# Bulk weights on ScalarE's DMA queue in fewer pieces, x first, another planned order, in a sliding-window attention block

## The chip, the cores and the metric

The kernel runs on 1 core of a Trainium2 chip, as one launch. The metric is the device time of that launch in microseconds (us), lower is better. The kernel before was run 13 times: median 338.93 us, from 337.63 to 341.28.

A core has five engines that run side by side, each through its own list of instructions, in order: TensorE (PE; its weight loads are listed as PEld), VectorE (DVE), ScalarE (ACT), GpSimd (POOL) and SyncE (SP). They wait for each other through semaphores. Transfers run on 16 DMA engines that the whole core shares; a transfer is started by an instruction in the list of SP or of ACT.

## The reference

All tensors are bf16. The sequence has 2048 rows of width 640; there are 32 heads of width 20, a causal window of 256, and an MLP of width 1536.

```python
mod = (_silu(c) @ w_mod).reshape(1, 6, 1, -1)   # c: (1, 640), w_mod: (640, 3840)
sa, ca, ga, sb, cb, gb = (mod[:, i] for i in range(6))
h = _layernorm(x) * (1 + ca) + sa
q, k, v = split_heads(h @ wqkv)                 # 32 heads of 20
scores = q @ k.T * 20 ** -0.5                   # row i sees columns i-255 .. i
x = x + ga * ((softmax(scores) @ v) @ wo)
h = _layernorm(x) * (1 + cb) + sb
x = x + gb * ((sigmoid(h @ w_gate) * (h @ w_up)) @ w_down)
```

## The kernel before

**Staging.** The sequence is cut into 8 chunks of 256 rows, each of two blocks of 128. For each chunk the kernel does the layernorm (`ln_stats`: two halves of statistics and an aggregation per block on VectorE, the reciprocal root on GpSimd, then the normalised x), a transpose of it to hT with the modulation, the products q, k and v (`qkv`), the attention (`score_set`, `burst`, `norm`), the output product (`outproj`), a second layernorm and transpose to h2T, and the MLP (`mlp`). Weights stay in SBUF for the whole run.

**The modulation.** w_mod comes in three parts of 1280 columns. They borrow the space of tensors that are needed later: part 0 lies in wd, part 1 in wu, part 2 in hh. So in the profile a transfer "wu<-in_w_mod" is part 1 of w_mod, and "hh<-in_w_mod" part 2. The vector c is loaded as a row, turned into a column by a small matmul (c_col), passed through tanh (cth) and multiplied to silu (siluc), and spread into silubc, the operand of the modulation's matmuls. Part 0 gives shift and scale of the first layernorm (mA); part 1 the gate of the attention (gbc, which is multiplied into wo) and a shift (shB); part 2 a scale (scB) and the gate of the MLP (gbc again, multiplied into wd).

**Attention.** For a chunk after the first there are 12 score sets, six for each half of the heads (chunk 0 has three for each half). A set is 8 or 16 small matmuls into the PSUM tile S, one exp on ScalarE over 128x2048 values into a tile E, and masks by GpSimd. There is one S, so the next set's matmuls wait for the exp. After the sets of a half come 64 matmuls E times V (`burst`; 32 for chunk 0), VectorE's transposes and division (`norm`: T, Dr, Tn, On), a write to a scratch tensor in DRAM (doc) and a read back (oT).

**Transposes.** Chunks 0 and 1 are transposed by matmuls with the identity (x to hT, stg to QT and KT). For the later chunks, and for h2T always, DMA transposes started by SP do it, and the modulation is applied afterwards by one of VectorE, ScalarE and GpSimd (`modulate`).

**What sets the order.** The code records operations with their reads, writes, allowed engines, planned durations and a priority (`Prog.op`). `Prog.schedule` then places them one after another on the engines by the earliest planned start; among those that could start within a small margin (PE_EPS on TensorE) the lowest priority number goes first. Where several engines are allowed it also chooses the engine. Priorities are a base plus an entry of the table PRI by a tag such as "score3". For transfers the planner keeps two queues' planned bandwidth and a planned landing time with an added latency `lat`. `Prog.emit` writes each engine's list in that order, with the semaphore waits. Nothing is moved at run time. So a changed duration, latency or priority changes the order on all engines.

**Loads.** `load_x` loads a block of x, `load_wm` a fifth of part 0 of w_mod, `load_w3` wq, wk or wv. `load_bulk` cuts a weight into at most BN pieces, and `chain` makes each piece wait for the landing of the piece DEEP places earlier. With BN = 5 and DEEP = 3 the parts 1 and 2 of w_mod, wg and wu come as five pieces each, on SP's queue (BQ = "sp"), wo as one piece and wd as four. Blocks 0 and 1 of x and the row c are started by ACT.

**Start of TensorE.** Before there is data, `warm` issues nine pairs of 512-column matmuls on zeros, and `fill` puts further ones between the five groups of part 0's matmuls and into the first transposes.

The normalised x (line 751) may be computed by VectorE or GpSimd (XHE), the modulation (lines 765 and 766) by VectorE, ScalarE or GpSimd (MOE). Line 658 is the helper `mm` that issues most matmuls, 659 the same with a tile position (attention), 536 the helper that starts a plain transfer, 757 the one that starts a transpose; 812 and 813 copy a PSUM result out on ScalarE and VectorE, 924 is the exp, 932 and 934 are the masks.

Of the kernel before, what the change touches and what calls it, by code (L numbers as in the profile page):

```python
# [394 lines left out]
def c_pe(n):  # L395
# [3 lines left out]
PE_EPS = 0.117  # L399
PRI = {  # L400
    "amodu2": 349.1, "amodu3": 69.8, "amodu4": -2, "amodu5": 20.4, "amodu6": 21.9, "amodu7": 33.4, "apow0": -17.1,
    "apow1": -0.2, "apow2": -233.1, "apow3": -9.4, "apow4": -4.7, "apow5": -39.6, "apow6": -201.2, "apow7": 26.9,
    "astats1": 2, "astats2": -137.3, "astats3": 147.7, "astats4": 52, "astats5": 202.7, "astats6": 112.2,
    "astats7": -8.8, "atr3": -6.2, "atr4": -3.2, "atr5": -194.6, "atr6": 10.3, "atr7": -24.5, "axh0": -203,
    "axh2": -66.7, "axh3": 71.6, "axh4": -24.4, "axh5": 33.9, "axh6": -20.5, "axh7": 9.8, "bmodu0": -166.8,
    "bmodu1": 13.9, "bmodu2": 1.5, "bmodu3": 15.4, "bmodu4": -1.8, "bmodu5": 93.1, "bmodu6": 3.4, "bmodu7": -1.2,
    "bpow0": 4.3, "bpow1": 150.8, "bpow2": -11.8, "bpow3": -188.6, "bpow4": -35, "bpow5": 41.6, "bpow6": -22.5,
    "bpow7": -15.1, "bstats0": 20.1, "bstats1": 21.9, "bstats2": 16.8, "bstats3": 14.9, "bstats4": 25.8,
    "bstats5": -84.4, "bstats6": 22.4, "bstats7": -22.6, "btr0": -39.2, "btr1": -39.3, "btr2": -8.5, "btr3": 35,
    "btr5": -82, "btr6": 4.1, "btr7": -2.4, "bxh0": 24.8, "bxh1": -260.1, "bxh2": -55.1, "bxh3": 34, "bxh4": 72.4,  # L410
    "bxh5": 103.8, "bxh6": 81, "bxh7": 17.1, "divide_0": -16.1, "divide_1": 34.3, "divide_2": -154.9,
    "divide_3": 6.6, "divide_4": 14.8, "divide_5": -19.9, "divide_6": -11.9, "divide_7": 6.6, "down0": -15.1,
    "down1": -21.3, "down2": -20, "down4": 0.4, "down5": 1.9, "down7": 60.2, "evqk0": 16.1, "evqk1": 334.5,
    "evqk2": 27.2, "evqk3": 339.9, "evqk4": -0.3, "evqk5": 4.1, "evqk6": -33, "evqk7": -0.3, "evqt0": -11.6,
    "evqt1": -8.4, "evv0": 41.8, "evv1": 235.3, "evv2": 2.5, "evv3": -5.5, "evv4": -16.9, "evv5": -108.2,
    "evv6": -60.1, "evv7": -59.5, "exp0": -116.1, "exp1": -16.2, "exp2": -46.3, "exp3": 5.9, "exp4": -147.4,
    "exp5": -3.4, "exp6": 1.1, "exp7": -126.7, "glu_0": -1.3, "glu_1": 0.5, "glu_2": 26.7, "glu_3": -19.5,
    "glu_4": -37, "glu_5": -3.6, "glu_6": 8.5, "glu_7": 4.2, "hTe0": -31.6, "hTe1": 34.3, "mask0": 136.2,
    "mask2": -61.4, "mask3": 78.7, "mask4": -36.4, "mask5": -30.5, "mask6": 3.2, "mask7": 94.8, "mlpg0": -25,
    "mlpg1": -24.5, "mlpg2": -24, "mlpu0": -25, "mlpu1": -24.5, "mlpu2": -24, "modb": -25.7, "modc": -22.2,  # L420
    "n_ow_0": -20.3, "n_ow_1": -41.5, "n_ow_2": 44.8, "n_ow_3": 103.9, "n_ow_4": -5.8, "n_ow_5": -19.8,
    "n_ow_6": -1.4, "n_ow_7": 33.8, "oT_0": 17.5, "oT_1": 32.5, "oT_2": 12.6, "oT_3": 76.6, "oT_4": -64.2,
    "oT_5": 13.2, "oT_6": 2.6, "oT_7": 49.3, "out": 7.2, "projk0": -33.4, "projk2": 26.4, "projk3": -3.9,
    "projk4": 15.6, "projk5": 1.5, "projk6": 7.4, "projk7": 4, "projq0": -114.6, "projq2": 45.3, "projq3": -8.2,
    "projq4": 6.1, "projq5": -4, "projq6": 8.5, "projq7": -7.9, "projv0": -43.1, "projv1": 8.7, "projv2": 224.6,
    "projv4": -6, "projv5": 2.7, "projv6": 16.2, "projv7": 10.7, "ptr0": -337.9, "ptr1": -256.9, "pv0": -37.3,
    "pv1": -290.4, "pv2": -37.9, "pv3": -37.1, "pv4": -28.1, "pv5": -70.8, "pv6": -10.1, "pv7": -9.1, "qkt2": 7.9,
    "qkt3": 6.7, "qkt4": 64.8, "qkt5": -12.3, "qkt6": -3.6, "qkt7": -4.9, "qtr0": -154.4, "qtr1": -20.9,
    "recip_1": -1.9, "recip_2": 23.6, "recip_3": -2.4, "recip_4": 28.1, "recip_5": -22.7, "recip_6": 2.1,
    "recip_7": -9.2, "res1_0": -0.2, "res1_1": 5, "res1_2": 55.2, "res1_3": 7.6, "res1_4": 13.1, "res1_5": -5.3,  # L430
    "res1_6": -6.4, "res1_7": 11.2, "res2_0": 6.2, "res2_1": -29.9, "res2_2": -5.9, "res2_3": 1.7, "res2_4": -3.1,
    "res2_5": 40.9, "res2_6": -17.8, "res2_7": 2.6, "score0": -287.1, "score1": -347.7, "score2": -20.2,
    "score3": 1.8, "score4": -13.1, "score5": -50.5, "score6": -2.7, "score7": 11.5, "tanh_0": 29, "tanh_1": 20.7,
    "tanh_2": 23.5, "tanh_3": 22.7, "tanh_4": 26.2, "tanh_6": -2.3, "tanh_7": -20.3, "tr1_0": 19.8, "tr1_1": 6.2,
    "tr1_2": -28.1, "tr1_3": 15.6, "tr1_4": 45.4, "tr1_5": -90.8, "tr1_6": -19.7, "tr1_7": 5.2, "tr2_0": 204.6,
    "tr2_1": 224.6, "tr2_2": -128.4, "tr2_3": 42, "tr2_4": 64.5, "tr2_5": 40.4, "tr2_6": 0.1, "tr2_7": 27.5,
    "wd": -19.6, "wds": -7.7, "wg": 2.8, "wm2": -13.2, "wo": -20, "wo0": -2.2, "wo1": -12.2, "wo2": 9.1, "wo4": 10.8,
    "wo5": 28.7, "wo6": 6.6, "wo7": 30, "wos": -29.2, "x10": 529.8, "x11": 584.9, "x12": 476, "x13": 633,
    "x14": 745.4, "x15": 731.1, "x4": 394.6, "x5": 337, "x6": 375.5, "x7": 0.5, "x8": 473.6, "x9": 471.4, "y0": 10.9,
    "y1": 23.7, "y10": 8.6, "y11": 0.3, "y12": 0.2, "y13": 31.2, "y14": 1, "y15": 2.7, "y2": -0.2, "y3": 0.4,  # L440
    "y4": 24.5, "y5": 24.4, "y6": 15.9, "y7": -3, "y8": 23.9, "y9": 2,
# [4 lines left out]
DEEP = 3  # L446
MW = 64
PACE0 = -95.83
PACE = 0.103
AFTER = 0  # L450
LEAD = 2
FILL = 1
WDG = 1
WSE = ("dve", "dve")
BQ = "sp"
BN = 5
# [3 lines left out]
XHE = ('dve', 'pool')  # L460
MOE = ('dve', 'act', 'pool')


def build(nc, A_x, A_wqkv, A_wo, B_x, B_w_gate, B_w_up, B_w_down, c, w_mod, out, S=2048):
# [50 lines left out]
    p_st = sbpool("st", 3, [128, 32], F32)  # L515
# [51 lines left out]
    def load_x(pool, b, prio, tmin=0.0, eng="sp"):  # L567
        t = Tile(pool, f"{pool.name}_{b}")
        dma(lambda: t.ap[:], lambda: x_flat[b * 128:(b + 1) * 128, :], 0.47 if b > 1 else 0.9, writes=[t.r()], prio=prio, tmin=tmin, tag=f"x{b}" if pool is p_x0 else f"y{b}",
            eng=eng, lat=0.05 if b > 1 else 1.2)  # L570
        return t
# [8 lines left out]
    def load_wm(i, kt, prio, tmin=0.0):  # L580
        if i:
            raise AssertionError
        return dma(lambda: wm_ap[i][:, kt, :], lambda: wm_src[:, kt, i * 1280:(i + 1) * 1280], (1.12 - 0.06 * kt if kt < 4 else 1.2), writes=[Rm[i][kt]],
                   prio=prio, tmin=tmin, tag=f"wm{i}")
# [15 lines left out]
    def load_w3(k, prio, halves):  # L600
# [6 lines left out]
        if k == "wk" and BQ != "sp":  # L607
            front.append(o)

    x0 = {}  # L610
    x0[0], x0[1] = load_x(p_x0, 0, 0, eng="act"), load_x(p_x0, 1, 0, eng="act")
    for kt in range(NDT):
        load_wm(0, kt, 0.2 + 0.01 * kt)
    load_w3("wq", 0.30, True)
# [567 lines left out]
```

The softmax here doesn't subtract the row's maximum and nothing guards it: scores larger than these inputs give would overflow.

## Time and profile before

| What | us |
|---|---|
| median of 13 runs | 338.93 |
| lowest, highest | 337.63, 341.28 |
| the profiled execution, its own time | 339.9 |
| its span, first to last instruction | 337.9 |
| ScalarE: 90 exps (line 924), mean of one | 168.9, 1.876 |
| VectorE: 64 statistics (line 741), mean of one | 28.3, 0.478 |
| VectorE: normalised x (line 751), 26 times, median and longest | 0.741, 1.371 |
| GpSimd: normalised x (line 751), 6 times, median | 2.510 |
| DMA: bytes moved | 38.73 MB, mean 115 GB/s |

A span is the time from the first to the last instruction in one profiled execution. A row of the timeline gives start, length, engine, line, operation, tiles (written <- read), shapes, a count of merged instructions, and in brackets the idle time of that engine just before, with what ended it. Matmuls are pipelined and the length of one matmul's row is its latency, so a TensorE that is called busy need not be at its peak. A row of the stages view gives the window, its length, then for PE, PEld, DVE, ACT and POOL the busy time and the count, then TensorE's granted clock, the busy share of the DMA engines and the GB/s moved. In the list of waits a row is: who waited, for whom, the sum in us, how often, and the longest.

### The profile page before, as it was taken

Reading aid. Unit: us, or ns where it says so; the run is one execution under the profiler, and the core shown is the slowest. Engines: PE = TensorE matmul, PEld = TensorE weight load, DVE = VectorE, ACT = ScalarE, POOL = GpSimd, SP = SyncE. Lnnn points to the kernel's source line nnn. Section 1 sums busy time; section 2 is a strip of 40 time slices with the busy share of each in tenths; the row PEclk is TensorE's granted clock in tenths of the full one; section 3 lists DMA queues with packets and bytes.
Section 4 is the critical chain, followed back from the end, with each engine's and each line's share of the span. In section 5 each row is a group of like instructions: output and inputs, shape, how many; then the busy total and the mean of one; then the engine's idle time right before and its main releaser. Section 6 shows DMA issues by size and latency. Waiting matters only on the chain.

```text
span 337.9 us, 10119 instructions
## 1 busy us (share of the span) xinstructions
PE 326.3 (97%) x4146; PEld 232.4 (69%) x4146; DVE 221.4 (66%) x441; ACT 229.9 (68%) x220; POOL 183.4 (54%) x255
## 2 busy tenths in 40 slices
PE   8986899899999999999999999999999999999996
PEld 3754555566776667766677666776677788887885
DVE  5586788789789767366898376844667662733332
ACT  1695699788988498968799779998699532230120
POOL 5137999775859686646686556665576610100000
PEclk9999999999999999999999999999999999999999
DMA  7986999677990287116761425200140221101101
GB/s 270 375 274 231 283 326 163 151 173 93 220 241 15 70 143 118 48 44 140 123 126 34 94 70 131 46 17 21 60 94 26 59 87 53 21 19 41 41 0 41
DMA packets 71687, 38.73 MB, mean 115 GB/s; under 512 B 46682, under 2 KB 68442, under 8 KB 71642
## 3 DMA queue, kind: packets, MB, share of 16 engines
q1 hardware_dynamic: 71344, 37.76, 45.7%
q8 instruction: 33, 0.54, 0.7%
q10 hardware_dynamic: 298, 0.33, 0.3%
q14 instruction: 12, 0.10, 0.1%
HBM read 21.96 MB, written 5.24 MB: 80 GB/s over the span
## 4 chain that ended last, share of the span: by engine, by line
PE 73%; DMA 9%; POOL 6%; SPq 3%; issue 3%; DVE 3%; ACT 1%; POOLq 0%; ACTq 0%
PE M L658 60%; PE S L659 7%; PE M L659 6%; SPq L536 3%; POOL E L934 2%; DMA wd<-in_B_w_down_dram 2%; DMA wv<-in_A_wqkv_dram 2%; POOL E L932 2%; DMA wo<-in_A_wo_dram 2%; POOL x L751 1%; DMA hh<-in_w_mod_dram 1%; ACT E L924 1%; DMA wu<-in_w_mod_dram 1%; DMA hT<-x 1%; DVE x L751 0%
## 5 line engine op out<-in xcount | busy, mean ns | idle before, releaser
L924 ACT ACTIVATE E<-S 128x2048 bf16<-128x2048 f32 x90 | 168.9, 1876 | 31.9 <-PE S L659 29.5
L932 POOL TENSOR_SCALAR_AFFINE_SELECT E<-E 128x512 bf16<-128x512 bf16 (+2 forms) x90 | 75.9, 844 | 73.5 <-ACT E L924 68.8
L934 POOL TENSOR_SCALAR_AFFINE_SELECT E<-E 128x512 bf16<-128x512 bf16 (+1 forms) x84 | 68.3, 813 | 0.0
L658 PE MATMUL M<-h2T,wg 128*128 128x256 bf16 x480 | 63.6, 273 | 0.1
L658 PE MATMUL M<-h2T,wu 128*128 128x256 bf16 x480 | 63.2, 273 | 0.0
L1080 DVE SCALAR_TENSOR_TENSOR hh<-sig,M 128x512 bf16<-128x512 f32 x48 | 32.5, 679 | 46.1 <-PE M L658 30.8
L1078 ACT ACTIVATE sig<-M 128x512 f32<-128x512 f32 x48 | 28.5, 594 | 43.9 <-PE M L658 43.9
L658 PE MATMUL M<-wd,hh 128*128 128x320 bf16 (+2 forms) x396 | 55.6, 295 | 0.0
L658 PEld LDWEIGHTS M<-h2T,wg 128*128 128x128 bf16 x480 | 45.0, 98 | 9.6 <-issue 2.7
L658 PEld LDWEIGHTS M<-h2T,wu 128*128 128x128 bf16 x480 | 45.9, 98 | 7.4 <-issue 1.7
L658 PEld LDWEIGHTS M<-wd,hh 128*128 128x128 bf16 x396 | 37.0, 98 | 15.4 <-issue 1.7
L659 PE MATMUL S<-QT,KT 20*128 20x256 bf16 (+1 forms) x960 | 35.9, 245 | 0.4 <-ACT E L924 0.4
L1099 DVE TENSOR_TENSOR x<-M,x 128x320 bf16<-128x320 f32 (+2 forms) x33 | 15.5, 477 | 22.4 <-PE M L658 22.4
L741 DVE BATCH_NORM_STATS2 st<-x 128x6 f32<-128x320 bf16 x64 | 28.3, 478 | 2.8 <-DMA x<-in_A_x_dram 2.4
L975 DVE STREAM_TRANSPOSE T<-M 128x512 f32<-128x512 f32 x32 | 21.2, 695 | 13.1 <-PE M L659 13.1
L659 PEld LDWEIGHTS S<-QT,KT 20*128 20x128 bf16 x960 | 14.1, 92 | 20.6 <-ACT E L924 16.3
L658 PE MATMUL M<-wk,hT 128*128 128x320 bf16 x160 | 25.9, 300 | 0.0
L659 PE MATMUL M<-E,V 128*32 128x256 bf16 (+1 forms) x960 | 22.7, 246 | 3.3 <-POOL E L934 1.5
L658 PE MATMUL M<-wq,hT 128*128 128x320 bf16 x160 | 25.6, 300 | 0.1
L659 PEld LDWEIGHTS M<-E,V 128*32 128x32 bf16 x960 | 20.0, 97 | 7.5 <-POOL E L934 2.7
L658 PE MATMUL M<-wv,hT 128*128 128x320 bf16 x160 | 25.1, 300 | 0.0
L658 PE MATMUL M<-wo,oT 128*128 128x320 bf16 x160 | 24.6, 300 | 0.0
(76 smaller groups left out, 321.3 us busy)
## 6 DMA issues: line engine op xcount, KB each, us to landing
x<-in_A_x_dram SPq DMA_DIRECT2D x30, 160.0 KB
doc<-On SPq DMA_DIRECT2D x64, 40.0 KB
out_dram<-x SPq DMA_DIRECT2D x15, 160.0 KB
wg<-in_B_w_gate_dram SPq DMA_DIRECT2D x5, 384.0 KB
wu<-in_B_w_up_dram SPq DMA_DIRECT2D x5, 384.0 KB
wd<-in_B_w_down_dram SPq DMA_DIRECT2D x4, 480.0 KB
wd<-in_w_mod_dram SPq DMA_DIRECT2D x5, 320.0 KB
wu<-in_w_mod_dram SPq DMA_DIRECT2D x5, 320.0 KB
```

Of the source, the lines that this page charges most:

```text
L536: return e.dma_start(dst(), src())
L658: return e.matmul(o, l, r, start=st, stop=sp, skip_group_check=True)
L659: return e.matmul(o, l, r, start=st, stop=sp, tile_position=tp, skip_group_check=True)
L741: A("dve", lambda e, g, bi=bi, j=j: e.bn_stats(v(bi * 12 + j * 6, 6), src[bi].ap[:, j * 320:(j + 1) * 320]), 0.48, reads=[src[bi].r()], wr ...
L751: A(XHE, lambda e, g, bi=bi: e.tensor_scalar(dst[bi].ap[:], src[bi].ap[:], v(24 + 2 * bi, 1), v(30 + bi, 1), op0=ALU.subtract, op1=ALU.mul ...
L924: A("act", lambda e, eng: e.activation(E.ap[:], Sp.ap[:], ACT.Exp, scale=SM_SCALE), 1.876, reads=[Sp.r()], writes=[E.r()], prio=3, tag=f"e ...
L932: return e.affine_select(ap, ap, pattern=[[0, ap.shape[1]], [1, 128]], compare_op=ALU.is_ge, fill=0.0, base=0, channel_multiplier=-1)
L934: return e.affine_select(ap, ap, pattern=[[0, ap.shape[1]], [-1, 128]], compare_op=ALU.is_ge, fill=0.0, base=-1, channel_multiplier=1)
L975: A("dve", lambda e, g, h=h: e.transpose(T1.ap[:, 512 * h:512 * h + 512], X[h].ap), 0.694, reads=[X[h].r()], writes=[T1.r(h)], prio=3.5, t ...
L1078: A("act", lambda e, g, pg=pg, sg=sg: e.activation(sg.ap[:], pg.ap[:], ACT.Tanh, scale=0.5), c_act(512), reads=[pg.r()], writes=[sg.r()], ...
L1080: A("dve", lambda e, g, pu=pu, sg=sg, f0=f0: e.scalar_tensor_tensor(out=hh.ap[:, f0:f0 + 2, :], in0=sg.ap[:].rearrange("p (a b) -> p a b", ...
L1099: A("dve", lambda e, g, ps=ps, bi=bi, c0=c0, n=n: e.tensor_tensor(x1[bi].ap[:, c0:c0 + n], ps.ap[:, 0:n], x1[bi].ap[:, c0:c0 + n], op=ALU. ...
```

## The change

These things change; what is computed stays the same.

- The table PRI gets other entries throughout, and the planner's constants change: PE_EPS from 0.117 to 0.187, PACE0 and PACE (earliest planned starts of score sets), the planned work and latencies of the loads, the planned durations of some VectorE and GpSimd operations. The order on all engines and the choice of engines follow from them.
- Bulk weights are started from ACT's list (BQ), parts 1 and 2 of w_mod, wg and wu in two pieces each (three fifths and two fifths), each piece waiting for the piece two places earlier (DEEP = 2); wo stays one piece, wd four. In all 13 bulk transfers stand in ACT's list.
- Blocks 0 and 1 of x are started first by SP, ahead of part 0 of w_mod.
- `warm` issues five pairs instead of nine; FILL is 2, so that two 512-column matmuls stand between the groups of part 0, and two in the transposes, as before.
- silubc is written in two halves of 64 columns; the second half is needed by `mod_bc` alone.
- The normalised x is computed by VectorE alone (XHE).

Counted in the built lists: TensorE issues 4142 matmuls where it issued 4146; 32 normalised x blocks are on VectorE where 26 were, and six fewer on GpSimd; of the modulations of h2T 14, 12 and 14 are on VectorE, ScalarE and GpSimd where 18, 14 and 8 were. On VectorE's list the statistics of blocks 0 and 1 now stand ahead of c_col and of most of the condition's chain. Chunk 0's last product columns of k now stand behind those of v and behind part 1's matmuls.

```diff
-PE_EPS = 0.117
+PE_EPS = 0.187
 PRI = {
...
 }
-DEEP = 3
+DEEP = 2
 MW = 64
-PACE0 = -95.83
-PACE = 0.103
+PACE0 = -145.28
+PACE = -6.585
-FILL = 1
+FILL = 2
-BQ = "sp"
-BN = 5
+BQ = 'act'
+BN = 2
-XHE = ('dve', 'pool')
+XHE = ("dve",)
...
     def load_x(pool, b, prio, tmin=0.0, eng="sp"):
         t = Tile(pool, f"{pool.name}_{b}")
-        dma(..., 0.47 if b > 1 else 0.9, ..., lat=0.05 if b > 1 else 1.2)
+        dma(..., 0.47, ..., lat=-0.7 if b > 3 else -0.4 if b < 2 else -1.0)
...
     x0 = {}
-    x0[0], x0[1] = load_x(p_x0, 0, 0, eng="act"), load_x(p_x0, 1, 0, eng="act")
+    x0[0], x0[1] = load_x(p_x0, 0, 0), load_x(p_x0, 1, 0.1)
...
-    A("dve", lambda e, g: e.tensor_copy(silubc[:], siluc[:].unsqueeze(2).to_broadcast([128, NDT, 128])), 0.8,
-      reads=[R_siluc], writes=[R_silubc], prio=0)
+    A("dve", lambda e, g: e.tensor_copy(silubc[:, :, 0:MW], siluc[:].unsqueeze(2).to_broadcast([128, NDT, MW])), 0.45,
+      reads=[R_siluc], writes=[R_silubc], prio=-1)
+    R_silub2 = R("silub2")
+    A("dve", lambda e, g: e.tensor_copy(silubc[:, :, MW:128], siluc[:].unsqueeze(2).to_broadcast([128, NDT, 128 - MW])), 0.45,
+      reads=[R_siluc], writes=[R_silub2], prio=6)
...
-    for i in range(9):
+    for i in range(5):
         o = A("pe", warm, 0.85 if i < 4 else 0.43, prio=90, reads=[R_z], extra=wprev, tag="warm", writes=[R("w")])
...
             if a == 0 and dt == 3:
-                fills.append(fill(2 * FILL, [o]))
+                fills.append(fill(FILL, [o]))
```

## The prediction

> **What bounds the kernel now.** I read the busy times first, then TensorE's own waits, the stages, and last the rows around each wait.
>
> ```profile
> PE 326.3 (97%) x4146; PEld 232.4 (69%) x4146; DVE 221.4 (66%) x441; ACT 229.9 (68%) x220; POOL 183.4 (54%) x255
> ```
>
> TensorE is the bound. Its instruction list is almost the same after the change: 4146 matmuls become 4142, the four fewer being warm-up ones. So only its waits can move the time, and the list of waits by engine says how much there is (waited for: total us, times, longest):
>
> ```profile
> PE M L658 <- DMA hh<-in_w_mod_dram: 2.0, 2, 1.4
> PE M L659 <- POOL E L934: 1.5, 1, 1.5
> PE S L639 <- DVE E L634: 1.3, 1, 1.3
> PE M L658 <- DVE stg L813: 1.3, 2, 0.9
> PE M L659 <- POOL E L932: 0.7, 1, 0.7
> ...
> ```
>
> All ten lines together are 8.7 us, of which 1.3 is the start. Where they lie, by stretches (PE, PEld, DVE, ACT, POOL busy):
>
> ```profile
> 24.00:40.00 16.00, 11.67 (x179) 7.28 (x178) 10.52 (x25) 9.60 (x10) 12.68 (x10) 1.00 0.88 250
> 40.00:62.00 22.00, 20.15 (x290) 12.71 (x290) 16.88 (x32) 19.70 (x21) 20.91 (x26) 1.00 0.95 241
> 120.00:270.00 150.00, 149.91 (x2100) 105.72 (x2101) 100.29 (x188) 126.46 (x102) 97.21 (x130) 1.00 0.37 77
> ```
>
> Before 24 us PE is nearly full but for the start, from 24 to 62 it is idle 6.2 us of 38, after 120 never: then the MLP's matmuls fill every hole. What is decided is decided before 120 us. What PE waited for in 24 to 62, from the chain that ended last and from the timeline (start, length; idle before in brackets):
>
> ```profile
> 10.01 7.23 DMA wv<-in_A_wqkv_dram
> 17.25 3.25 DMA wu<-in_w_mod_dram
> 20.52 6.60 DMA wo<-in_A_wo_dram
> 27.13 4.71 DMA hh<-in_w_mod_dram
> ```
>
> ```profile
> 25.55 0.40 PE L658 MATMUL M<-ident,stg 128*128 128x128 bf16 x4 [0.94 <-DVE stg L813]
> ...
> 31.89 0.32 PE L658 MATMUL M<-silubc,hh 128*128 128x64 bf16 x5 [1.43 <-DMA hh<-in_w_mod_dram]
> ...
> 49.69 5.00 POOL L751 TENSOR_SCALAR x<-x,st 128x640 bf16<-128x640 bf16 x2
> ...
> 60.22 1.50 PE L659 MATMUL M<-E,V 128*32 128x256 bf16 x64 [1.46 <-POOL E L934]
> ```
>
> One chain of weight pieces, each issued when an earlier one lands, ends at 31.85 with the third part of w_mod. Then POOL, which normalises two x blocks at 2.5 us each (49.69 to 54.7) ahead of its masks; the attention matmul at 60.22 waits for these masks.
>
> **The change, part by part.** The sum is a difference to the profiled execution: span 337.9, run 339.9 (2.0 lies around the span), which is 1.0 above the median of 338.93. I apply the difference to the median.
>
> *A, head: +0.8.* Rows of the head:
>
> ```profile
> 1.37 0.84 ACTq L536 DMA_DIRECT2D x<-in_A_x_dram  x2
> ...
> 3.51 1.87 PE L639 MATMUL S<-E 128*128 128x512 bf16 x4
> ...
> 4.26 0.82 DVE L630 COPY silubc<-siluc 128x640 bf16<-128x640 bf16 x1
> 5.18 0.89 DVE L741 BATCH_NORM_STATS2 st<-x 128x6 f32<-128x320 bf16 x2
> ...
> 9.90 0.17 DVE L729 COPY mA<-S 128x10 f32<-128x10 f32 x1 [0.33 <-PE S L658]
> ```
>
> x blocks 0 and 1 (0.33 MB) now come first. At 0.23 MB in 2 to 3 us and 0.37 MB/us after that they land at about 3.4, where VectorE waited for them until 5.2 and 6.5; I take 3.2 for the first and 3.6 for both. But VectorE's list now has the statistics of both ahead of the condition: 4 x 0.445 + 0.2 (BATCH_NORM rows) = 2.0, so c_col at 5.2, ScalarE's tanh and siluc 0.7 (3.62 to 4.26 in the trace), half of silubc 0.41: the first modulation matmul starts at about 6.4 against 5.22. From there PE's list holds five groups of 0.29, ten fills of 0.216 and eight transposes of 0.45 in all before the last group ends: 4.1, so 10.5 and not 9.70. From the last group to the first wq matmul (mA, then the first hT evacuations) the trace has 1.2 (9.70 to 10.91), and the same steps stand there afterwards. First wq matmul: 11.7 against 10.91, +0.8. Warm-ups are ten instead of 18, yet the matmuls that cost are the fills behind the condition. Bounds: -0.5 (the first group starts at 5.2 as before, and hT's evacuations overlap its fills) and +1.2 (x lands 0.4 later).
>
> *B, two queues: +0.4.* wv landed at 17.24. TensorE wants it 5.2 of matmuls and 0.3 of evacuations after the first wq: 17.2. The first piece of wu (960 KB) now enters on ScalarE's queue at about 14.5, beside wv. None to 2.0 (wv's tail at half rate); I stay near none, since most of wv has moved by then at 0.36 to 0.39 MB/us.
>
> *C, weights of the modulation: -2.0.* The waits for hh (0.59 and 1.43), stg3 behind x's landing (0.94) and one of 0.31 are 3.3. Bytes up to hh's end are the same, some 9.5 MB (9280 KB); at 0.36 MB/us from 2.0 they need 26 us, so 28.5 against 31.85, if the engines never idle. GB/s of 253 to 307 between 16 and 32 says that they do now, because five pieces each wait for the third last. Two pieces of 960 and 640 KB cure part of it. Ends 0 and -3.3; I take -2.0.
>
> The Trainium skill, DMA: Bandwidth & Descriptors, section "Issuing engines are not separate DMA queues", speaks against it: whichever engine starts a transfer, it runs on the same 16 DMA engines, and only the issuing sequencer's time is saved. By it C is zero and the sum -0.5. The rows, 253 to 307 GB/s there against 387 at 12 to 16 us, show transfer engines that idle between pieces, so C goes by them.
>
> *D, normalising on VectorE alone: -1.8.* Six POOL rows of 2.51 go; the waits of 0.74 (39.1) and 1.46 (60.22) behind them, 2.2, go too. VectorE gets 6 x 0.74 (its median) = 4.4 more over 30 to 110 us; where it is 92% busy (62 to 86) a tenth of that is on the path, 0.4. Bounds -2.7 and +0.5.
>
> *E, issues on ScalarE: +0.4.* Thirteen bulk DMAs come, two x leave. At 0.42 each (two in 0.84) they hold ScalarE 5.5. Nine stand before the exps of chunk 1, where ScalarE's idle brackets between 22 and 41 us add up to 6.7 (1.66, 1.72 and 1.47 the largest); four with wd at 80 to 90, where the MLP covers. What waits behind an issue is an evacuation or an exp, and TensorE behind that. If that cover is gone, up to +3.0 (the second hh piece waits for wo's landing).
>
> *F, new places to wait: +0.7.* I count both orders of PE with the spacing of neighbouring matmuls in long runs (0.136, 0.109 and 0.056 us for 320, 256 and 128 columns): the MLP of chunk 0 starts after 68.1 us of matmuls instead of 71.6, and between the last wo matmul and it lie 11.4. In the trace wo ends at 71.2, h2T's last modulation at 85.7: 14.5, with slack I can't see. None to +3.1; nearer none, for wo itself stands behind 1 us less of matmuls. SP has 23 issues fewer to go past, so the transposes aren't later there.
>
> *G, other order: -1.0.* The small waits left (0.23, 0.39, 0.53, 0.54 and 0.3 of hT) are 2.0; half. Tail and MLP stage: nothing, PE has no hole after 120 us.
>
> Sum: 0.8 + 0.4 - 2.0 - 1.8 + 0.4 + 0.7 - 1.0 = -2.5. Median 338.93 - 2.5 = **336.4** (span 335.4).
>
> **Rivals.**
>
> *R1, slower: ScalarE becomes the gate.* From 41 to 62 us it is busy 19.7 of 22 and TensorE's scores come one per exp, 2.46 apart. An issue that waits for a landing holds everything behind it. wo took 6.6 from issue to landing; if it takes as long after exp 1, the second hh issue, two evacuations behind it, blocks 2 to 3, and the 5.5 of issues are no longer hidden. Cost 7 instead of 0.4: +4.1, 343.0. It decides from 2.9 lost on ScalarE on (2.5 and the 0.4 counted). For it: the busy time; against: the brackets of 6.7 before 41. 0.22.
>
> *R2, no change: given back at h2T.* What is won before 62 us is waited for at the first gate matmul, since chunk 0's chain through VectorE (92% busy) and the transposes sets its start: F at its bound of 3.1 instead of 0.7, sum -0.1, 338.8. For it: 14.5 against 11.4; against: the slack in the 14.5. 0.17.
>
> *R3, all waits go.* The ten waits less the start, 7.4, and A at -0.5: 7.9 less, 331.0. For it: they all lie behind things the change touches; against: new orders bring waits of their own. 0.13.
>
> That the change doesn't do what it says: the weights need as long as before, C = 0. That alone gives 338.4 and is within the forecast's range.
>
> **How the numbers follow.** Forecast 0.48, R1 0.22, R2 0.17, R3 0.13. About 0.3% (1.0 us) is what a measurement can tell. Faster: 0.40 of the forecast, R3, 0.03 of R2: 0.56. Same: 0.06 of the forecast and 0.11 of R2: 0.17. Slower: R1, 0.02 and 0.03: 0.27. The forecast's own range, with one of C, E or F at its end, is 333.7 to 339; to leave out no more than 2 in 10 it goes down to R3, 331.0, and up to R1, 343.0.
>
> **What would show it.** A: first wq matmul at 11.7. B: a wait for wv on PE. C: hh's last landing before 30, and no PE wait for it over 0.5. D: no POOL row on line 762, PE's wait for masks gone. E: ScalarE's queue waiting for landings less than 1 in all. F: a PE wait at the first h2T,wg. I am wrong if PE's waits before 120 us add up to more than before, above all for exp.

## The result, and the profile after

The changed kernel takes 349.32 us (median of 11 runs, 345.28 to 352.9), against 338.87 for the kernel before (48 runs): ratio 1.0245, 95% interval 1.0213 to 1.0277. It is 2.45% slower, 13 us above the forecast and outside its range. Here and below, a ratio leaves out runs that took over 1.5% more than the fastest run of the same kernel, a median does not. The profiled execution, with 352.9, is the slowest of the changed kernel's runs; its span is 350.8, 12.9 more than the span of 337.9 before.

First the page of the changed kernel, busy times and two of the rows of 40 slices, each 8.8 us long:

```profile
PE 331.3 (94%) x4142; PEld 233.9 (67%) x4142; DVE 224.9 (64%) x448; ACT 227.6 (65%) x216; POOL 172.9 (49%) x253
...
PE   7876949999989999999999999999999999999997
...
PEclk9998896999999999999999999999999999999999
```

No engine is busy for over 5 us more than before, and GpSimd for 10 us less. TensorE has holes in the first six slices (53 us) and in the twelfth, and its granted clock, 9 in every slice before, falls in slices 4, 5 and 7. Two stages of the view by windows (window, length, then busy time and count of PE, PEld, DVE, ACT, POOL, granted clock, DMA share, GB/s):

```profile
24.00:40.00 16.00, 12.72 (x126) 7.98 (x124) 9.71 (x26) 6.84 (x7) 4.61 (x5) 0.79 0.78 262
40.00:62.00 22.00, 16.34 (x225) 10.05 (x222) 13.27 (x27) 14.36 (x15) 10.99 (x14) 0.84 0.70 181
```

Before, TensorE got 179 and 290 matmuls done in these two windows; now 126 and 225. VectorE, ScalarE and GpSimd do less in them too (ScalarE 6.84 and 14.36, against 9.60 and 19.70), so none of them is short of time. The transfer engines move about as much as before in the first and less in the second (262 and 181 GB/s against 250 and 241). TensorE's waits of the changed kernel (waited for: total us, times, longest):

```profile
PE M L660 <- POOL hT L778: 5.2, 1, 5.2
PE S L661 <- DVE KT L825: 3.3, 1, 3.3
PE S L661 <- ACT E L936: 2.0, 2, 1.6
PE M L660 <- DMA wv<-in_A_wqkv_dram: 1.5, 1, 1.5
```

The old waits, for hh (2.0) and for masks (1.5 and 0.7), are gone as planned. Two long ones have come, 5.2 and 3.3, each once. Where they come from is in the timeline (start, length; idle before in brackets with what ended it):

```profile
23.65 0.80 SPq L535 DMA_DIRECT2D x<-in_A_x_dram  x2
...
23.97 0.40 ACTq L535 DMA_DIRECT2D hh<-in_w_mod_dram  x1
...
28.14 0.89 DVE L743 BATCH_NORM_STATS2 st<-x 128x6 f32<-128x320 bf16 x2 [1.57 <-DMA x<-in_A_x_dram]
28.39 0.44 PE L660 MATMUL M<-wq,hT 128*128 128x320 bf16 x2
30.97 0.49 DVE L743 BATCH_NORM_STATS2 st<-x 128x6 f32<-128x320 bf16 x1 [1.94 <-DMA x<-in_A_x_dram]
31.38 0.67 DVE L825 CAST KT<-M 128x512 bf16<-128x512 f32 x1
...
32.11 0.61 PE L661 MATMUL S<-QT,KT 20*128 20x128 bf16 x16 [3.28 <-DVE KT L825]
...
41.50 3.69 SPq L769 DMA_TRANSPOSE hT<-x  x2
42.72 1.15 ACTq L535 DMA_DIRECT2D wu<-in_B_w_up_dram  x2
48.77 4.37 SPq L535 DMA_DIRECT2D x<-in_A_x_dram  x4
51.86 1.09 ACT L777 ACTIVATE hT<-hT,mA 128x256 bf16<-128x256 bf16 x2 [4.86 <-DMA hT<-x]
...
53.10 1.25 PE L660 MATMUL M<-wk,hT 128*128 128x320 bf16 x4 [5.23 <-POOL hT L778]
```

At 28: VectorE stands at the statistics of a block of x that has not landed, and behind them in its list is the copy of KT that the next scores need. That block, the second of the two issued from 23.65, was issued 0.1 us behind hh's first piece (960 KB) on the other ring (the queue of the other issuing engine) and landed 6.9 us later, at 30.9. At 42: the two hT transposes (in the new order chunk 3's, which come first) are issued by SP, and w_up's two pieces (1920 KB) by ScalarE right after the first. The modulation can start at 51.9, 10.4 us after the first transpose was issued. The kernel before needs 8.2 us from its first hT transpose (33.26) to its first modulation (41.46), with pieces of wg in between. In all VectorE waits 11.6 us for x, where it waited 2.4 before.

And each long hole is followed by something that no list of waits shows. Windows of 2 us of the same execution, the granted clock third from the end:

```profile
30.00:32.00 2.00, 0.00 (x0) 0.00 (x0) 1.03 (x3) 0.00 (x0) 0.00 (x0) 0.90 0.73 277
32.00:34.00 2.00, 1.89 (x22) 1.12 (x23) 2.00 (x8) 1.23 (x1) 0.00 (x0) 0.50 0.21 47
36.00:38.00 2.00, 2.00 (x19) 0.98 (x17) 0.53 (x2) 0.57 (x1) 1.62 (x3) 0.50 0.83 336
...
50.00:52.00 2.00, 0.00 (x0) 0.00 (x0) 0.00 (x0) 0.14 (x1) 0.05 (x1) 1.00 1.00 197
54.00:56.00 2.00, 1.97 (x9) 0.82 (x8) 1.94 (x3) 1.14 (x3) 1.97 (x4) 0.50 0.29 89
58.00:60.00 2.00, 2.00 (x13) 1.16 (x10) 1.38 (x4) 1.47 (x2) 0.80 (x1) 0.77 0.98 118
```

From 32.1 to 38.4 and from 53.1 to 58.9 TensorE works at half its clock: 12.1 us of work that would take an estimated 6.0 at full clock. So the balance of this execution is: new waits 5.2 + 3.3 + 1.5 (wv) + 1.6 (exp, 2.0 against 0.4) + 1.1 (start) = 12.7; half clock 6.0; old waits gone, hh 2.0, masks 2.2, stg behind x 1.3, together 5.5. Sum 13.2, seen 12.9.

The half clock is not special to the slowest execution. The mean granted clock on record is 0.980 to 0.990 in every run of the changed kernel: 0.990 in those of 345.3 to 345.8 us, 0.985 in those of 347.1 to 349.5, 0.980 or 0.981 in those above 351. Where the holes lie is known for this one execution alone.

### The profile page after: what moved, and what is told of

The parts are those of the page before. It is cut to its first block, busy times and chain, and to the rows that moved or that the text cites. A ratio compares the mean times of both kernels' runs of the same rounds, so it can differ in the third digit from the quotient of the medians.

```text
span 350.8 us, 10080 instructions
## 1 busy us (share of the span) xinstructions
PE 331.3 (94%) x4142; PEld 233.9 (67%) x4142; DVE 224.9 (64%) x448; ACT 227.6 (65%) x216; POOL 172.9 (49%) x253
## 4 chain that ended last, share of the span: by engine, by line
PE 79%; DMA 10%; SPq 3%; issue 3%; DVE 2%; ACT 0%; POOL 0%; ACTq 0%; DVEq 0%
PE M L660 66%; PE S L661 7%; PE M L661 6%; SPq L535 3%; DMA x<-in_A_x_dram 3%; DMA wd<-in_B_w_down_dram 2%; DMA wv<-in_A_wqkv_dram 2%; DMA hT<-x 2%; DMA h2T<-x 1%; DVE x L762 1%; SPq L769 0%; DVE x L1050 0%; ACT sig L1090 0%; DVE hT L799 0%; POOL hT L778 0%
## 5 line engine op out<-in xcount | busy, mean ns | idle before, releaser
L944 POOL TENSOR_SCALAR_AFFINE_SELECT E<-E 128x512 bf16<-128x512 bf16 (+2 forms) x90 | 76.9, 854 | 89.1 <-ACT E L936 86.0
L1092 DVE SCALAR_TENSOR_TENSOR hh<-sig,M 128x512 bf16<-128x512 f32 x48 | 32.6, 681 | 49.2 <-PE M L660 38.2
L660 PE MATMUL M<-h2T,wg 128*128 128x256 bf16 x480 | 62.2, 273 | 0.7 <-DVE x L1050 0.3
L743 DVE BATCH_NORM_STATS2 st<-x 128x6 f32<-128x320 bf16 x64 | 28.4, 477 | 12.0 <-DMA x<-in_A_x_dram 11.6
L660 PE MATMUL M<-wk,hT 128*128 128x320 bf16 x160 | 27.7, 318 | 5.7 <-POOL hT L778 5.2
L660 PE MATMUL M<-wq,hT 128*128 128x320 bf16 x160 | 27.1, 314 | 0.3
L660 PEld LDWEIGHTS M<-wk,hT 128*128 128x128 bf16 x160 | 15.4, 103 | 14.3 <-POOL hT L778 5.5
```

The source lines that it names most:

```text
L660: return e.matmul(o, l, r, start=st, stop=sp, skip_group_check=True)
L743: A("dve", lambda e, g, bi=bi, j=j: e.bn_stats(v(bi * 12 + j * 6, 6), src[bi].ap[:, j * 320:(j + 1) * 320]), 0.48, reads=[src[bi].r()], wr ...
L944: return e.affine_select(ap, ap, pattern=[[0, ap.shape[1]], [1, 128]], compare_op=ALU.is_ge, fill=0.0, base=0, channel_multiplier=-1)
L1092: A("dve", lambda e, g, pu=pu, sg=sg, f0=f0: e.scalar_tensor_tensor(out=hh.ap[:, f0:f0 + 2, :], in0=sg.ap[:].rearrange("p (a b) -> p a b", ...
```

## The experiments

Theories. **T1**: the transfers of the two rings run on the same engines, roughly in the order in which they are issued, so a bulk piece on ScalarE's ring holds up a small transfer on SP's; VectorE's and TensorE's fixed lists turn that into idle time. **T2**: the new planned order is at fault by itself. **T3**: part of the loss is the clock after each hole. **R1**, the prediction's rival: ScalarE is held up by issuing.

A changed constant would have re-planned the whole kernel. So the experiments leave the plan as it is and move single operations in the finished lists, between `P.schedule()` and `P.emit()`, with two helpers: `at(P, e, tag, t)` is the operation of that tag on engine e whose planned start is nearest t, and `put(P, ops, ref)` takes operations out of their lists and sets them ahead of ref. The semaphore waits are written afterwards from the same dependences.

**1. KT ahead of the statistics** (kt_first, from the changed kernel).

```diff
+put(P, [at(P, "dve", "evqt0", 24.55)], at(P, "dve", "astats2", 23.34))
```

> The changed kernel with one step moved in its finished order: VectorE copies KT out ahead of the three statistics that wait for x, not behind them. Theory T1 (x lands late, and VectorE, which works its list in order, makes TensorE wait for a copy that was ready): KT copied at about 28.2 us instead of 31.4, score set 3 at 28.9 instead of 32.1, the idle time of 3.45 us there under 0.7, and the ten wq matmuls behind it in about 1.5 us instead of 2.85. In all 3 to 5 us faster than the changed kernel's 349.3: 344.5 to 346.5. Rival (x's landing rules the next steps anyway, the time is only waited for later): the gap goes, but the one at 47.7 grows by as much, 348.5 to 350.

Measured: 351.8, ratio 1.0369 (1.03 to 1.0439). Its waits on TensorE:

```profile
PE M L660 <- POOL hT L778: 4.5, 1, 4.5
PE S L661 <- ACT E L936: 3.7, 2, 3.3
PE M L660 <- DVE shB L1131: 3.1, 1, 3.1
```

The wait for KT is gone, and a wait of 3.1 for shB, the next thing behind the statistics in VectorE's list, has taken its place; the clock fell as before. T1's gain of 3 to 5 failed, and the ratio lies above the changed kernel's 1.0245: a copy moved ahead of a late transfer cures nothing while the rest of the list still stands behind it. The transfer has to come earlier. The wait of 3.3 for an exp, at 102.8, has another cause, which experiment 6 comes to: on ScalarE this exp stood 4.3 us behind an issue of wd that waited for a landing.

**2. w_up behind the transposes, and bulk weights back on SP** (wu_late, bulk_on_sp).

```diff
+put(P, wu, at(P, "act", "amodu3", 38.52), after=True)    # wu_late: both pieces of w_up
```

```diff
+for o in [o for o in P.order["act"] if o.isdma and o.tag != "dma"]:    # bulk_on_sp
+    put(P, [o], next(x for x in P.order["sp"] if x.start > o.start))
```

> The changed kernel with the two pieces of w_up (1920 KB) issued by ScalarE two modulations later in its list, so behind the landing of the hT transposes. T1 (transfers on ScalarE's ring slow the transposes on SP's): the second hT transpose lands within 4 us of its issue instead of 8.0, the idle 5.41 us of TensorE before wk,hT is under 1.5, total 4 to 6 us less than 349.3: 343.5 to 345.5. Rival T2 (the planned order is at fault, whatever runs beside it): the transposes still need 7 us or more, total within 1 of 349.3.

> The changed kernel's order, with all 13 bulk transfers issued by SP instead of ScalarE, at the places in SP's list that their planned times give. T1: in one ring the hT transposes go out ahead of w_up, so the idle time before wk,hT shrinks from 5.4 to under 1.5, while the one behind x's landing (28.7) stays: 343.5 to 346. T2 (order alone): 348.5 to 350. R1 of the prediction (ScalarE is held up by issuing): everything from the first bulk piece on is earlier by 2 to 3, the gap at 28.7 too.

Measured: 343.73 (1.0155, 1.008 to 1.0231) and 343.16 (1.0158, 1.0077 to 1.024), outside what T2 allows and at T1's times (bulk_on_sp 0.3 below them). By the ratios that is 3 us of the 8.3 that the changed kernel loses, by the medians 5.6 and 6.2 of 10.4. The longest wait for hT is under 1 us in both. In these two profiled executions x was also issued 0.4 ahead of hh's first piece, landed at 27.1 instead of 30.9, and the hole at 28 was 1.1 and 1.2 us. In bulk_on_sp the one list puts x ahead, and T1's forecast that this hole stays was wrong. In wu_late it is luck, since nothing there differs from the changed kernel up to that point. Its four runs fit a race that is won in half of them: 342.0 and 342.1 at a mean granted clock of 1.00, 345.3 and 346.6 at 0.990 and 0.985; only one of them was traced. As wu_late has the short hole with the issues still on ScalarE, the hole says nothing for R1. bulk_on_sp paid 3.6 at another place (KT, behind blocks of x that now stood behind w_up on SP).

**3. The other way round: bulk weights of the kernel before on ScalarE** (before_bulk_on_act, and once more for its trace).

```diff
+for o in [o for o in P.order["sp"] if o.tag in ("wm1", "wm2", "wo", "wg", "wu", "wd")]:
+    put(P, [o], next(x for x in P.order["act"] if x.start > o.start))
```

> The kernel before, order and pieces as they were, with its 25 bulk transfers issued by ScalarE instead of SP, at the places that their planned times give. T1: the hT transposes of chunk 2 land 2 us or more later after their issue than before, and TensorE waits for hT: 3 to 8 us slower, 342 to 347. R1: as slow, but with TensorE waiting for ScalarE (evacuations, exp) and ScalarE's list waiting for landings by 3 or more. T2 (order alone): within 1 of 338.9.

> The same kernel as before_bulk_on_act, once more for its trace. T1: 343 to 346; the hT transposes issued at 33 to 36 us land over 5 us after their issue, and TensorE's idle time before 62 us is 5 us more than before. R1: ScalarE's list waits for landings by 3 us or more in all, and TensorE for ScalarE's evacuations or exps.

Measured: 345.5 (1.0175, 1.0114 to 1.0237), and 344.64 in the second, the only run of it. So the ring alone, with the old order and the old five pieces, costs some 6 us: not T2. But the place was not the expected one. hT's first modulation comes 7.9 us after the transpose is issued, against 8.2 before, and TensorE's idle time before 62 us grew by 0.7, not 5 (8.6 against 7.9; by 1.8 more up to 120). What grew is VectorE's wait for x, and behind one of these waits TensorE has a new one, for KT:

```profile
DVE st L741 <- DMA x<-in_A_x_dram: 6.6, 4, 2.4
```

```profile
PE S L659 <- DVE KT L813: 2.1, 1, 2.1
```

The wait for x is 6.6 against 2.4 before. The list of ScalarE's waits shows none for a weight's landing in that trace, and TensorE's waits for ScalarE add up to 0.9, so R1 does not explain it either. The span of this execution is 3.3 us longer than before, half of the 6; that the late x makes the whole loss is argued, not shown.

**4. hh behind x** (hh_late), **and both moves** (hh_wu_late).

```diff
+put(P, [at(P, "act", "wm2", 21.91)], at(P, "act", "evqk0", 23.25), after=True)    # hh_late
```

> The changed kernel with the first piece of part 2 of w_mod (hh, 960 KB) issued by ScalarE one evacuation later. In the changed kernel's run it was issued at 23.97, a block of x by SP at 24.07, and x landed 6.9 us after its issue, behind hh; in the two runs where x was issued 0.4 ahead of hh, it landed after 4.5. T1 (transfers of both rings are served in the order in which they were issued, so a bulk piece that gets in first delays a small one): now x is always ahead, lands before 28.5, the idle time at 28.7 (3.45) is under 1.5, the granted clock stays at 1.00 from 30 to 40 us, and the total is 345 to 347 with the gap at wk,hT still there. Rival (x is late for another reason, such as the late wv): x still lands after 30 in a run where wv lands after 18.5, 349 to 350.

> Both moves together: hh's first piece one evacuation later, w_up's two pieces behind the landing of the hT transposes. T1: all runs like the better ones of w_up alone, 341 to 343, with TensorE at full granted clock from 10 us on. Rival: the spread of w_up alone (342.0 to 346.6) stays, since it comes from something else.

Measured: hh_late 348.29 (1.0238, 1.0148 to 1.0327), hh_wu_late 340.27 (1.0032, 1.0004 to 1.006; 339.41 to 341.37 in ten runs). In hh_late x is issued at 24.3 and hh at 27.2, the hole at 28 shrank to 0.8 us, and the clock stayed at 1.00 from 30 to 40, as T1 said. But the total missed the 345 to 347: in the profiled execution, the slowest of the four with 356.5, the time won was lost again at hT, with a wait of 10.3 us instead of 5.2. With w_up also moved, both waits are under 1 us, and by the ratios 7.2 of the 8.3 us are back (by the medians 9.0 of 10.4). hh_wu_late in the timeline:

```profile
37.12 2.93 SPq L769 DMA_TRANSPOSE hT<-x  x2
41.40 1.76 SPq L535 DMA_DIRECT2D x<-in_A_x_dram  x4
42.23 1.10 POOL L778 TENSOR_SCALAR hT<-hT,mA 128x256 bf16<-128x256 bf16 x2
42.29 0.41 ACTq L535 DMA_DIRECT2D wu<-in_B_w_up_dram  x1
```

From 37.12 to 42.23 is 5.1 us. The same distance, read from the timelines of all runs of the changed plan that show it:

| Run | first hT transpose issued | w_up's pieces issued | first modulation of hT | distance, us |
|---|---|---|---|---|
| changed kernel | 41.5 | 42.7, 43.5 | 51.9 | 10.4 |
| kt_first | 39.9 | 41.1, 41.9 | 49.6 | 9.7 |
| hh_late | 38.3 | 39.6, 42.2 | 54.1 | 15.8 |
| fill_gap | 35.2 | 36.4, 38.4 | 49.2 | 14.0 |
| fill_more | 41.1 | 42.3, 43.1 | 50.9 | 9.8 |
| wu_late | 35.8 | after | 40.9 | 5.1 |
| bulk_on_sp | 35.3 | 38.7, same ring | 40.4 | 5.1 |
| hh_wu_late | 37.1 | after | 42.2 | 5.1 |

5.1 where w_up stands behind both transposes, 9.7 to 15.8 where it is issued between or right behind them on the other ring. This is the clearest number of the study.

**5. The clock** (fill_gap, fill_more).

```diff
+def fill(e, g):                   # 18, then 40 times; the product that follows overwrites ps
+    for i in range(18):
+        ins = e.matmul(ps.ap[:, 0:512], ident[:], wq[:, 0, 0:512], start=True, stop=True)
+P.order["pe"].insert(P.order["pe"].index(at(P, "pe", "projk3", 38.55)), f)
```

> The changed kernel with 18 matmuls of 512 columns (3.9 us), whose result is overwritten, put on TensorE ahead of the wk,hT product that waits for POOL's modulation at 47.7. Nothing else moves, the wait stays. T3 (half of the loss is the clock: after an idle stretch of 3 us or more TensorE runs at a granted clock of 0.50 for some 6 us): granted clock 1.00 from 52 to 60 us instead of 0.50, and 2.5 to 3.2 us less: 346 to 347. Rival (the clock is granted by something else, or what waits there is not TensorE): clock or time as in the changed kernel, 348.5 to 350.

> The changed kernel with 40 matmuls of 512 columns (8.6 us) instead of 18 ahead of the wk,hT product, since the wait there turned out to be 9 us long in all: 3.9 under the 18, and 5.1 idle, after which the clock fell to 0.50 all the same. The result of the 40 is overwritten and the wait for hT stays as it is. T3 (the clock falls after an idle stretch of 3 to 4 us, and costs some 3 us more): no idle stretch over 2.5 us there, granted clock 1.00 from 40 to 62 us, 2 to 3.5 us less than with 18: 345 to 346.5. Rival (the clock has another cause): it falls to 0.50 again, 348 to 349.5.

Measured: 348.44 (1.0275, 1.0222 to 1.0329) and 349.69 (1.0264, 1.0198 to 1.0331). With 18 the wait outlasted the filling by 4.9 us and the clock fell to 0.50 at about 49.4. With 40 it did not fall there:

```profile
50.00:54.00 4.00, 4.00 (x20) 1.84 (x19) 1.19 (x4) 3.10 (x4) 3.01 (x6) 1.00 0.54 140
54.00:58.00 4.00, 4.00 (x39) 2.18 (x36) 2.44 (x5) 0.63 (x3) 1.66 (x2) 1.00 0.08 28
```

So the hole makes the clock fall (T3). The time that this saves was not shown, and both forecasts of the total (346 to 347, 345 to 346.5) were missed: in the profiled execution hT was ready at about 52 and the 40 ran until 56.0, which costs as much as the clock would have. A filling of fixed length does not fit a wait of 5 to 10 us.

**6. Curing the early race without delaying hh, the start, and a buffer** (best2, best2_head, best2_x15).

```diff
+put(P, [at(P, "sp", "x5", 20.38), at(P, "sp", "x6", 20.83)], at(P, "act", "wm2", 21.91), eng="act")
+put(P, wu, at(P, "act", "amodu3", 38.52), after=True)
+put(P, [at(P, "dve", "evqt0", 24.55)], at(P, "dve", "astats2", 23.34))
+put(P, [x0, x1 loads], P.order["act"][0], after=True, eng="act")       # best2_head, too (this and the next lines shortened)
+put(P, [c_col, siluc, both silubc], at(P, "dve", "astats0", 2.4))
+put(P, [x4 load], x15's place); put(P, [x15 load], at(P, "sp", "x12", 55.66))    # best2_x15, too
```

> The changed kernel with three moves: the loads of two blocks of x (the ones issued at 23.7 and 24.1) issued by ScalarE just ahead of hh's first piece, so that no race decides; w_up's two pieces behind the landing of the hT transposes; KT's copy on VectorE ahead of the statistics that wait for x. T1: no idle stretch of TensorE over 1.5 us before 110 us, clock 1.00 throughout, hh no longer late as in hh_wu_late (1.5 there): 338.5 to 340. Rival: the planned order has costs of its own that no landing explains, 340.5 or more.

> best2, with the start as in the kernel before: blocks 0 and 1 of x issued by ScalarE behind c, so that part 0 of w_mod comes first on SP, and the condition's chain (c_col, siluc, silubc) on VectorE ahead of the statistics of these blocks. Term A of the prediction (the new start costs 0.8, 1.1 measured): first wq matmul at 10.9 to 11.2 instead of 12, total 0.7 to 1.1 less than best2. Rival (the start is not on the path, wv's landing decides next): first wq earlier, the wait for wv longer by as much, total the same within 0.3.

> best2, with block 4 of x loaded early in place of block 15, which the changed kernel's plan loads at 12.7 us and keeps in one of four x buffers until chunk 7; block 15 is loaded behind chunk 2's transposes, its statistics stand with block 14's. T2 (part of the loss is the plan itself, which holds a buffer for 100 us): VectorE's waits for x between 40 and 60 us go, 0.5 to 1.5 us less than best2. T1 (these waits were only late landings and best2 has cured them): within 0.4 of best2.

Measured: best2 341.98 (1.0046, 1.0009 to 1.0084), best2_head 340.99 (1.0032, 0.9991 to 1.0072), best2_x15 342.64 (1.0072, 1.0035 to 1.0109). best2 missed T1's 338.5 to 340: its rival, a cost that no landing explains, had 340.5 or more. The buffer held for 100 us by block 15 costs nothing that can be seen. The old start did not bring the first wq product to 10.9: it came at 13.5, since the order puts transposes of x ahead of part 0's last group on TensorE, and they waited 2.1 us for the normalised x. The total did not suffer, so the start of the changed kernel is at most a small part of its loss. best2's own profile had one hole of over 2 us left, 2.3 us from 91.2, with this on ScalarE and TensorE (timeline):

```profile
85.95 0.37 ACTq L535 DMA_DIRECT2D wd<-in_B_w_down_dram  x1
...
91.06 0.37 ACTq L535 DMA_DIRECT2D wd<-in_B_w_down_dram  x1
91.56 1.88 ACT L936 ACTIVATE E<-S 128x2048 bf16<-128x2048 f32 x1 [3.30 <-DMA wd<-in_B_w_down_dram]
...
93.49 0.61 PE L661 MATMUL S<-QT,KT 20*128 20x256 bf16 x8 [2.30 <-ACT E L936]
```

The fourth piece of wd, next to issue, waits for the landing of the second, and an exp behind it waits 3.3 us: R1's mechanism, at 88 instead of at 41. kt_first and hh_late have the same, longer (4.3 and 4.5 us on ScalarE, 3.3 and 3.5 on TensorE, then half clock). In the changed kernel ScalarE idles for 2.6 us ahead of the same issue, at 102.1, and the exp behind it, most likely for the same landing.

**7. wd's fourth piece two exps later** (hh_wu_wd, best2_wd).

```diff
+put(P, [at(P, "act", "wd", 82.95)], at(P, "act", "exp2", 88.26))
```

> hh_wu_late (340.27; exp held 0.79 us there by the landing of a wd piece) with the fourth piece of wd issued by ScalarE behind two more exps and their sigmoids, so that the piece it waits for has long landed. If the wait on ScalarE is on the path: no exp after a landing of wd, 339.3 to 340. Rival: the same as hh_wu_late within 0.3.

> best2 (341.98; exp held 3.30 us there, then the clock at 0.50 for 3.4 us) with the same move of wd's fourth piece. If this wait makes the slower group of its runs: all runs in 338.5 to 340.5, clock 1.00, median 339.5. Rival (the two groups come from the start or from the early landings): the spread of 339.4 to 346.5 stays.

Measured: 340.23 (0.9999, 0.9962 to 1.0037) and 339.61 (1.0015, 0.9981 to 1.0048), without a wait for wd on ScalarE and at full clock in both profiles. For best2 the median fell by 2.4 and the highest run from 346.47 to 342.39, so most of the spread went, though not all: 338.5 to 340.5 was expected. For hh_wu_late, where the wait was only 0.8, nothing can be told apart. So the cost that best2's rival claimed is largely this wait. **Four moved operations (hh, w_up twice, wd) make the changed plan as fast as the kernel before; none of the versions is faster than that.**

**8. Terms D and C by themselves, in the kernel before** (before_xh_dve, before_two_pieces, before_both).

```diff
+for o in [o for o in P.order["pool"] if o.tag[1:3] == "xh"]:    # before_xh_dve
+    put(P, [o], next(x for x in P.order["dve"] if x.start >= o.start), eng="dve")
```

before_two_pieces joins pieces 1 to 3 and 4 to 5 of both parts of w_mod, of wg and of w_up to one transfer each, every bulk transfer waiting for the one two places earlier.

> The kernel before with one part of the change: the six normalisations that GpSimd does go to VectorE, at the places that their planned times give, the rest of the order kept. Term D of the prediction: TensorE's wait for masks of 1.46 us at 60.2 and that of 0.74 at 39.1 go, VectorE's longer list gives 0.4 back: 1.8 us faster, 336.5 to 338 (bounds -2.7 and +0.5). Rival: VectorE's extra work delays its evacuations by as much, within 0.5 of 338.9.

> The kernel before with another part of the change: parts 1 and 2 of w_mod, wg and wu in two transfers each (three fifths and two fifths), each waiting for the piece two places earlier, all on SP's queue in the old order. Term C of the prediction: hh's last piece lands before 30 instead of 31.85, TensorE's waits for hh (2.0 in all) shrink to 0.5: 1 to 2 us faster, 337 to 338. Rival (the transfer engines had no idle time to win, and a matmul now waits for three fifths where it waited for one): hh lands no earlier than 31.5, and the time is the same or up to 1.5 longer.

> Both parts in the kernel before. If the terms C and D hold and add up: 335 to 337, better than both kernels. Rival: within 0.7 of 338.9.

Measured: 340.64 (1.0054, 1.0024 to 1.0084), 342.85 (1.0105, 1.0067 to 1.0144), 343.48 (1.0116, 1.0071 to 1.0162). Both terms have the wrong sign, and together they come to no gain either. TensorE's waits in before_xh_dve:

```profile
PE M L658 <- issue: 2.0, 1, 2.0
PE S L639 <- DVE E L634: 1.3, 1, 1.3
PE M L659 <- DVE gbc L706: 1.2, 1, 1.2
```

The mask waits are gone, but the first wo product, which reads oT, starts after a hole of 2.0 for which the profile names no cause, and an E times V product waits 1.2 for VectorE: the 2.2 us came back as 3.2. In before_two_pieces the waits and two windows:

```profile
PE M L658 <- DMA hh<-in_w_mod_dram: 2.8, 1, 2.8
```

```profile
30.00:32.00 2.00, 1.68 (x11) 1.11 (x12) 0.00 (x0) 0.40 (x1) 2.00 (x1) 0.50 0.30 68
32.00:34.00 2.00, 2.00 (x24) 1.07 (x23) 0.24 (x1) 0.81 (x2) 1.83 (x3) 0.50 0.96 344
```

One wait of 2.8 stands where two of 0.6 and 1.4 stood, since the first matmul needs three fifths where it needed one, and the hole is long enough for the clock to fall: it stays at 0.50 for 6.8 us, which costs up to an estimated 3.4. hh's second and last piece landed at 31.78. The 31.85 that the prediction reads as the end of hh in the kernel before is the landing of the third of five pieces, issued at 27.13; two more follow. By the semaphore events of the traces the last of the five landed at 33.38 there, and at 31.90 in before_xh_dve, whose loads are the same. So bigger pieces brought the end of hh forward by 0 to 1.6 us, and the time did not follow it.

**9. The rest of the changed plan's loss** (three_moves: hh_wu_late and the move of 1).

> hh_wu_late (340.27) with KT's copy on VectorE ahead of the statistics that wait for x. If the wait for KT (0.83 us at 28 in hh_wu_late) is on the path: 339.3 to 339.8. Rival (the wait for hh 2 us later takes its place): 340 to 340.6.

Measured: 340.66 (1.0042, 1.0012 to 1.0071): the rival. The wait for KT was not on the path.

## Why the prediction was wrong

The step that failed is the pricing of the second queue, B, together with the sentence in F that the transposes aren't later because SP has fewer issues to go past. B looked at the issuing side alone and charged the new ring only for wv's tail. The transfer side was the side that mattered: hT's transposes took 10.4 us from issue to use instead of 5.1 in the same plan without w_up beside them, x took 6.9 us beside hh, and both stand ahead of TensorE. hh's place and w_up's together cost 7.2 of the 8.3 us by the ratios, 9.0 of the 10.4 by the medians (349.3 to 340.3). w_up's place alone comes to 3.0 or 5.6, in runs some of which were also lucky with x.

- **A**: wq began at 12.02 (forecast 11.7). Right in size; its weight on the total was not shown to be more than a fraction.
- **B**: TensorE waited 1.5 for wv, inside the bounds of 0 to 2.0. That bulk pieces meet x and the transposes further on was not looked for.
- **C, -2.0**: wrong in sign, +3.6 when made alone. Bigger pieces brought hh's end forward by at most 1.6 us, not by the 3.4 at C's end, and a piece of three fifths is waited for as a whole: a hole of 2.8 and the half clock behind it. The 31.85 that C starts from was also not the end of hh (experiment 8). The Trainium skill (DMA: Bandwidth & Descriptors, "Issuing engines are not separate DMA queues") says that transfers of all issuing engines end up on the same 16 DMA engines. C set that rule aside for the rows of GB/s. Experiments 2 to 4 agree with it: the second queue by itself won nothing, and moving the bulk to it cost some 6 us in the kernel before.
- **D, -1.8**: the waits for masks went, as said, but the term is +1.4 alone: other waits came, 1.2 us of them for VectorE. The changed plan with the four moves still has C and D in it and takes as long as the kernel before, so its loss is mostly not theirs.
- **E, +0.4, and R1**: issuing costs ScalarE nothing that can be seen up to 62 us, where it now idles. R1 had the right mechanism at the wrong place and was not the main cause: one exp held by wd's landing at 88 to 105 us. That is 1.6 us on TensorE in the changed kernel's trace, up to 3.5 in other runs of its plan, and 2.4 in best2's median. Its time, 343.0, was still the nearest of the four, by luck.
- **F**: no wait of note at the first gate product; the chain before it was late as a whole.
- **G, -1.0**: not seen; the new order brought waits of its own.
- **Missing altogether**: that a long wait costs more than its length. Two holes of 5.2 and 3.3 us were followed by half clock worth an estimated 6.0. No term had that.

The test named at the end, TensorE's waits before 120 us above those of before, is the one that shows it (16.2 against 8.7 by the lists of waits); the cause named with it, exp, is 2.0 us of them. What stays open: why best2_wd still runs up to 342.4, and how much the clock alone costs, since the filling that was to measure it did not fit.

## What to carry to other kernels

A second issuing queue gave no second set of transfer engines here: before moving bulk transfers to it, list each small transfer on the other queue that something waits for, and see to it that none is issued just behind, or just ahead of, a large piece. Where the lists are fixed, let the order hold them apart (the bulk issue behind the consumer of the small transfer) instead of a race between two engines' issues. And price a TensorE hole of about 2 us or more at its length plus 1.7 or 3.4 us of half clock (estimated from stretches of 3.4 and 6.8 us at 0.50), so several short waits are better than one long one of the same sum.

## What the hardware showed

- **Transposes and row copies mixed are slow together.** In hh_late, with hT's transposes (256 byte packets) and w_up (3072 byte packets) interleaved, the engines moved 114 and 83 GB/s from 40 to 44 us at a busy share of 1.25 and 1.23; w_up nearly alone went at 342 GB/s from 46 to 48.
- **A small load beside a large piece of the other ring is late, and more so behind it.** x (160 KB) landed 6.9 us after its issue when it was issued 0.1 behind hh's first piece (960 KB), 4.5 when 0.4 ahead. The two share the engines rather than go strictly in turn: in the first case hh's piece was complete at 32.2 by the trace's semaphore events, 1.2 us after x.
- **The granted clock fell to 0.50 for 3.4 us or a multiple of it.** Each stretch at 0.50 in the traces lasted 3.41 us (best2, best2_x15, bulk_on_sp), 6.83 (both of the changed kernel, before_two_pieces) or 10.24 (hh_late, TensorE idle for 6.3 of it). After single holes it began 2.1 to 4.7 us after TensorE went idle, sometimes when work had already resumed, and ended 3.1 to 6.3 us after work resumed. Every single hole of 2.3 us or more led to it. Below that it was open: one of 1.84 (before_both, next line) did, one of 2.12 (before_bulk_on_act2) did not.

```profile
71.08 4.08 PE L658 MATMUL M<-wo,oT 128*128 128x320 bf16 x17 [1.84 <-issue]
```

  The Trainium skill (TensorE: Matmul & The Clock Gate, Part 1) gives a free-running window of about 3.4 us for both directions. The steps of 3.41 agree with it; the holes of 1.84 and 2.3 that led to half clock are shorter than one window, and the way back often took two.
- **One execution of before_bulk_on_act took 646.45 us**, the others 343 to 346: every matmul at double spacing throughout (222 ns where 109 is usual, for 256 columns), while the profile shows a granted clock of 1.00. Its median above contains it. No run explains it.
